# The first half of a unit's values rounded in two pieces around the next unit's first snapshot

## The chip, the cores and the metric

The kernel runs on one core of one Trainium2 chip. The metric is the device time of one execution in microseconds (us), as the median of several runs. Five engines work side by side, each through its own list of instructions in order: TensorE (PE in the rows; its weight loads are listed apart as PEld), VectorE (DVE), ScalarE (ACT), GpSimd (POOL) and SyncE (SP), which issues transfers.

## The reference

Attention with a squared rectifier, gated by `u`, is followed by two networks of two matrix products each:

```python
scores = (1.0 / S) * np.matmul(z, z.transpose(0, 2, 1))
x = u * np.matmul(np.maximum(scores, 0.0) ** 2, v)        # 2 x 3008 tokens, 256 wide
h = x @ w_in1;  g = h - np.tanh(h);  x = g @ w_out1       # 256 -> 2048 -> 256
h = x @ w_in2
g = np.where(h >= 1, h, np.where(h <= -1, 0.0, (h + 1) ** 2 / 4))
out = g @ w_out2
```

All 6016 tokens pass through both networks. The kernel's inputs are float32 (the weights of the networks arrive as float64 and are converted in the kernel).

## The kernel before, in words

After the attention both networks are worked off in units. A unit `(net, s, f)` belongs to one supertile `s` (1024 tokens, 896 in the last of six, so halves of 512 or 448 tokens) and to one of eight blocks `f` of 256 hidden features. There are 95 units, the first network's 48 ahead of the second's 47; each is one call of `Unit.emit(p)`, where `p` is the unit before. The order in which the code calls the engines is the order in which they work; nothing reorders it.

A unit makes its hidden values h with seven products instead of eight (a Strassen scheme on 2x2 blocks). Each product is three matmuls (`mult`), since every operand is held as a rounded part (`hi`) and a rest (`lo`). The seven are named in the code by their weight block: A11 and later S2, S3 and A22 are accumulated into one PSUM bank `Y`, A12 goes to `X`, S1 and S4 to `V`. Because `Y` goes on accumulating, ScalarE copies it out between products: the snapshots m1 (after A11), u2 (after S2) and u3 (after S3), all made by `snap`, shown in the trace as `m<-m` (m1) and `u<-m` (u2, u3). VectorE adds them up into h of the two halves: `ha` (first element: m1 and X; second: u3 and V) and `hb`.

Each half (class `Half`; `A` is the first, `B` the second) then goes through: `first` (in the first network the tanh, on ScalarE, tile `ta` or `tb`), `value` (on VectorE, h minus tanh, into the same tile), `round` (on ScalarE, `gha` or `ghb`, the rounded part), `rest` (on VectorE, `gla` or `glb`, the rounding's remainder). The second product (L828, `acc<-gha` and so on) is done one unit later, in pieces between the next unit's seven products, so that TensorE has work while the other engines prepare. The order on TensorE within a unit, three weight loads and matmuls for each product: A11, A12, S1, S2, then 8 with p's `gha` (4 on its element 0, 4 on its element 1), S3, 4 with `gla`, 6 with `ghb`, A22, S4, 2 with `ghb`, 4 with `glb`: 45 in all.

S2 has to wait until m1 has been copied out of `Y`, A22 until u3 has been, S4 until VectorE has read `V` (the add into `ha`'s second element).

In between, VectorE and ScalarE also do work for later: the operands of the next supertile (`xhb`, `xht`, `xhc` and their rests `xl`, the differences `t`, by `fill`), and the conversion of the next weights (`min`, `ein`, `win`, `phin`, `plin` and the like, by `work`).

A second-network unit is `late`: it rounds `gha` in the next unit, behind m1. In the first network `gha` is rounded at the unit's end (`self.A.round()`), ahead of the next unit's m1. At the second network's last supertile (`narrow`), `B.round` is made in two pieces, one ahead of u3 and one behind it; but in the second unit of that supertile (`before`, where the supertile before is also emptied) both pieces stand ahead of u3.

The line numbers are those of the profile.

Of the kernel before, what the change touches and what calls it, by code (L numbers as in the profile page):

```python
# [22 lines left out]
QT = 512  # L23
# [8 lines left out]
def attention_then_two_ffn(  # L32
# [72 lines left out]
    def flush():  # L105
        for fn in deferred:
            fn()
        deferred.clear()
# [614 lines left out]
    def fill():  # L723

        if fills:
            step = fills.pop(0)
            for fn in step:
                if fn is not None:
                    fn()
            if len(step) == 1:  # L730
                work(CONVERT[1] / 2)
        else:
            work(CONVERT[1])
        due()

    def copy(out_, in_):
        nc.scalar.activation(out=out_, in_=in_, func=AF.Copy)  # L737

    def add(out_, x, bank):
        nc.vector.tensor_tensor(out=out_, in0=x, in1=bank, op=ALU.add)  # L740
# [54 lines left out]
    class Unit:  # L795
# [60 lines left out]
        def emit(self, p, att=None):  # L856

            w = self.w
            before = p and p.net == 1 and p.f == 0 and p.s and p.before
            self.before = p  # L860
            self.late = self.net == 1 or att is not None
            one, two, three = p.parts_list if p else ([], [], [])
            narrow = self.net == 1 and w < QT
            Y = self.bank()
            self.mult(Y, A11, "b11", True)
            split = p and p.net == 1 and p.w < QT
            border = p and p.net == 1 and p.f == 0 and not before
            tight = border or narrow
            if split:
                p.A.round((0,))  # L870
            m1 = self.snap("m1", Y)
            if p and p.late:
                p.A.round((1,) if split else (None,), more=split)
            if p and p.before and p.before.net == 0:
                p.before.empty(0, leave=(1, 1) if p.net == 1 else None)
            X = self.bank()
            self.mult(X, A12, "b21", True)
            if p:
                if p.net == 1:
                    p.B.first()  # L880
                    if p.before and p.before.net == 0:
                        p.before.empty(0, late=((1, 1),))
                p.A.rest()
                p.B.first() if p.net == 0 else p.B.square(1 if before else None)
            if att:
                for fn in att[2][:5]:
                    fn()
            self.A = Half(self.net, w, "a")
            if not (p and p.late):
                add(self.A.h[:, 0, :w], m1, X[:, :w])  # L890
            V = self.bank()
            self.mult(V, S1, "t1", True)
            if att:
                for fn in att[2][5:]:
                    fn()
                got = []
                inside.append(lambda: self.mult(Y, S2, "t2"))
                inside.append(lambda: got.append(self.snap("u2", Y)))
                att[0]()
                u2 = got[0]  # L900
            else:
                if split and not before:
                    for fn in one[:2]:
                        fn()
                    one = one[2:]
                self.mult(Y, S2, "t2")
                u2 = self.snap("u2", Y)
            if before:
                before.empty(1, lambda: p.B.square(0), after=int(narrow))
            if p:  # L910
                for j in (1, 0) if before or border else (None,):
                    p.B.value(j)
                if p.late:
                    add(self.A.h[:, 0, :w], m1, X[:, :w])
            for fn in one[:4] if before else one:
                fn()
            if p:
                opening = before or p.net == 0 and p.f == 0 and p.w < QT
                p.B.round((1, 0) if opening else (1,) if tight else (None,))
                if self.i <= 1:  # L920
                    scales.pop()()
                    due()
                    due()
                elif not tight:
                    fill()
                if not tight:
                    p.B.rest()
            self.mult(Y, S3, "t3")
            if before:
                for fn in one[4:6] + two[:2] + one[6:]:  # L930
                    fn()
                two = two[2:]
            u3 = self.snap("u3", Y)
            if tight and not opening:
                p.B.round((0,), more=True)
            add(self.A.h[:, 1, :w], u3, V[:, :w])
            if border:
                p.B.rest()
            if self.net == 1 or att:
                self.A.first()  # L940
            if narrow:
                p.B.rest((1, 0))
            for fn in two:
                fn()
            if att:
                self.A.value()
                att[1]()
            if self.i > 1:
                fill()
            if self.net == 1:  # L950
                self.A.square()
            self.mult(Y, A22, "t4")
            self.mult(V, S4, "b22")
            self.B = Half(self.net, w, "b")
            if self.net == 0 and not att:
                self.A.first()
            copy(self.B.h[:, 1, :w], Y[:, :w])
            if not att:
                for j in (0, 1) if narrow else (None,):
                    self.A.value(j)  # L960
            if att:
                flush()
            add(self.B.h[:, 0, :w], u2, V[:, :w])
            for fn in three:
                fn()
            if not self.late:
                self.A.round()
            if p and p.net == 1:
                p.empty(0)
            self.parts_list = self.parts()  # L970
# [178 lines left out]
    with tc.manual_schedule():  # L1149
# [130 lines left out]
        def due():  # L1280

            now = [fn for k, fn in later if k <= 0]
            later[:] = [(k - 1, fn) for k, fn in later if k > 0]
            for fn in now:
                fn()
# [73 lines left out]
        p = None  # L1359
        for i, (net, s, f) in enumerate(units):  # L1360
            if f == 0:
                more = (net, s + 1) if (net, s + 1, 0) in units else (1, 0) if net == 0 else None
# [9 lines left out]
            p = u  # L1372
# [69 lines left out]
```

## Time and profile before

| what | value |
|---|---|
| time, median of 3 runs (lowest, highest) | 1417.55 us (1416.68, 1418.51) |
| the profiled execution's own time | 1418.15 us |
| its span, first to last instruction | 1416.4 us |
| TensorE, share of the span busy | 100% |
| TensorE weight loads | 83% |
| VectorE | 88% |
| ScalarE | 71% |
| GpSimd | 8% |
| granted TensorE clock, mean | 1.000 |

The busy share of an engine is a mean over the attention, the first network and the second. [...]

### The profile page before, as it was taken

Reading aid. Unit: us, or ns where it says so; the run is one execution under the profiler, and the core shown is the slowest. Engines: PE = TensorE matmul, PEld = TensorE weight load, DVE = VectorE, ACT = ScalarE, POOL = GpSimd, SP = SyncE. Lnnn points to the kernel's source line nnn. Section 1 sums busy time; section 2 is a strip of 40 time slices with the busy share of each in tenths; the row PEclk is TensorE's granted clock in tenths of the full one; section 3 lists DMA queues with packets and bytes.
Section 4 is the critical chain, followed back from the end, with each engine's and each line's share of the span. In section 5 each row is a group of like instructions: output and inputs, shape, how many; then the busy total and the mean of one; then the engine's idle time right before and its main releaser. Section 6 shows DMA issues by size and latency. Waiting matters only on the chain.

```text
span 1416.4 us, 21868 instructions
## 1 busy us (share of the span) xinstructions
PE 1410.3 (100%) x8206; PEld 1174.9 (83%) x8206; DVE 1246.1 (88%) x1574; ACT 999.7 (71%) x1273; POOL 116.6 (8%) x170
## 2 busy tenths in 40 slices
PE   9999999999999999999999999999999999999998
PEld 7888888888888888888888889988888888888897
DVE  8889899788898989899889889989898898988887
ACT  8888758888766767667676767666666666666764
POOL 0112110022110010110201110000000000000000
PEclk9999999999999999999999999999999999999999
DMA  8789897599989557484937567572564653546632
GB/s 228 247 281 260 228 239 191 179 282 273 257 215 324 198 193 253 170 306 134 332 129 289 212 230 270 169 294 89 176 226 178 208 191 102 188 161 219 236 103 43
DMA packets 228986, 301.02 MB, mean 213 GB/s; under 512 B 110576, under 2 KB 165616, under 8 KB 228880
## 3 DMA queue, kind: packets, MB, share of 16 engines
q1 hardware_dynamic: 212032, 257.87, 57.6%
q0 software_dynamic: 11552, 41.03, 8.2%
q10 hardware_dynamic: 5296, 0.72, 0.3%
q8 instruction: 64, 1.05, 0.3%
q14 instruction: 42, 0.34, 0.1%
HBM read 225.77 MB, written 73.79 MB: 212 GB/s over the span
## 4 chain that ended last, share of the span: by engine, by line
PE 98%; SPq 1%; DVE 0%; ACT 0%; DMA 0%; issue 0%
PE acc L828 36%; PE m L809 32%; PE acc L537 17%; PE acc L526 7%; PE sc L449 4%; SPq L397 1%; PE acc L1063 0%; PE h L1011 0%; PE acc L532 0%; PE warm L1147 0%; DMA ub<-in_u_dram 0%; PE acc L554 0%; DVE am L416 0%; DVE lo L499 0%; DVE lo L434 0%
## 5 line engine op out<-in xcount | busy, mean ns | idle before, releaser
L809 PE MATMUL m<-xht,w 128*128 128x512 f32 (+1 forms) x760 | 231.5, 386 | 0.0
L828 PE MATMUL acc<-ghb,w 128*128 128x512 f32 (+1 forms) x760 | 201.2, 386 | 0.0
L537 PE MATMUL acc<-hi,v 64*128 64x512 f32 (+1 forms) x1588 | 195.4, 382 | 0.1
L828 PE MATMUL acc<-gha,w 128*128 128x512 f32 (+1 forms) x760 | 188.0, 386 | 0.0
L537 PEld LDWEIGHTS acc<-hi,v 64*128 64x128 f32 x1588 | 148.5, 184 | 28.8 <-DVE y L592 0.8
L828 PEld LDWEIGHTS acc<-ghb,w 128*128 128x128 f32 x760 | 141.6, 188 | 28.8 <-ACT ghb L737 0.2
L828 PEld LDWEIGHTS acc<-gha,w 128*128 128x128 f32 x760 | 142.6, 188 | 27.4
L809 PEld LDWEIGHTS m<-xht,w 128*128 128x128 f32 x760 | 142.7, 188 | 26.7
L809 PE MATMUL m<-xlt,w 128*128 128x512 f32 (+1 forms) x380 | 147.3, 388 | 0.0
L782 DVE TENSOR_TENSOR gla<-ta,gha 128x1024 fp32r<-128x1024 f32 (+1 forms) x95 | 114.3, 1204 | 37.4 <-ACT gha L737 36.9
L737 ACT ACTIVATE ghb<-tb 128x1024 fp32r<-128x1024 f32 (+3 forms) x108 | 101.4, 944 | 59.7 <-DVE tb L768 59.2
L768 DVE TENSOR_TENSOR ta<-ha,ta 128x1024 f32<-128x1024 f32 (+2 forms) x102 | 114.4, 1127 | 27.4 <-ACT ta L764 22.3
L737 ACT ACTIVATE u<-m 128x512 f32<-128x512 f32 (+1 forms) x190 | 110.5, 581 | 30.9 <-PE m L809 30.0
L782 DVE TENSOR_TENSOR glb<-tb,ghb 128x1024 fp32r<-128x1024 f32 (+3 forms) x102 | 114.5, 1128 | 15.1 <-ACT ghb L737 14.8
L737 ACT ACTIVATE gha<-ta 128x1024 fp32r<-128x1024 f32 (+2 forms) x101 | 100.1, 991 | 38.3 <-DVE ta L768 37.9
L768 DVE TENSOR_TENSOR tb<-hb,tb 128x1024 f32<-128x1024 f32 (+3 forms) x101 | 114.8, 1137 | 7.2 <-ACT tb L753 2.6
L809 PE MATMUL m<-xhb,w 128*128 128x512 f32 (+1 forms) x380 | 115.7, 386 | 0.0
L537 PE MATMUL acc<-lo,v 64*128 64x512 f32 (+1 forms) x772 | 104.8, 382 | 0.2 <-DVE lo L434 0.2
L475 ACT ACTIVATE r<-sc 128x1024 f32<-128x1024 f32 (+1 forms) x83 | 84.4, 1017 | 28.7 <-PE sc L449 28.3
L764 ACT ACTIVATE ta<-ta 128x1024 f32<-128x1024 f32 (+1 forms) x47 | 49.1, 1046 | 78.6 <-DVE ta L755 78.6
L828 PE MATMUL acc<-gla,w 128*128 128x512 f32 (+1 forms) x380 | 101.5, 386 | 0.0
L828 PE MATMUL acc<-glb,w 128*128 128x512 f32 (+1 forms) x380 | 101.5, 386 | 0.0
(139 smaller groups left out, 2569.8 us busy)
## 6 DMA issues: line engine op xcount, KB each, us to landing
w<-packed SPq DMA_DIRECT2D x288, 512.0 KB, 5.9
mir<-ax SPq DMA_DIRECT2D x50, 512.0 KB, 4.6
m<-mir SPq DMA_DIRECT2D x200, 128.0 KB, 4.7
xr<-kept SPq DMA_DIRECT2D x20, 512.0 KB, 6.8
packed<-phin POOLq DMA_DIRECT2D x16, 512.0 KB, 5.8
packed<-plin POOLq DMA_DIRECT2D x16, 512.0 KB, 6.2
widein<-in_moe_w_in_dram POOLq DMA_DIRECT2D x15, 512.0 KB, 6.4
wideout<-in_moe_w_out_dram POOLq DMA_DIRECT2D x15, 512.0 KB, 7.4
```

Of the source, the lines that this page charges most:

```text
L397: nc.sync.dma_start(out=m[32 * i : 32 * i + 32, :k].rearrange("b k t a -> b k (t a)"), in_=src[:, :k, 256 * i + 128 * h : 256 * i + 128 * ...
L449: nc.tensor.matmul(ps[:, j, :n], zs[b, g][half, x, k0 : k0 + P], q[half, y, :n], start=(k == 0), stop=(k == 2))
L475: nc.scalar.activation(out=r[s], in_=ps[s], func=AF.Relu)
L526: nc.tensor.matmul(acc[d][h].rearrange("p (i q) -> p i q", i=2), lhsT, g[half, j], start=start, stop=stop)
L537: nc.tensor.matmul(acc[d][h][:, :n], lhsT, g[half, j, :n], start=start, stop=stop and (h == 1 or not closes))
L737: nc.scalar.activation(out=out_, in_=in_, func=AF.Copy)
L764: nc.scalar.activation(out=t, in_=t, func=AF.Square, scale=0.5, bias=0.5)
L768: nc.vector.tensor_tensor(out=t, in0=self.h[self.at(j)], in1=t, op=ALU.subtract if self.net == 0 else ALU.max,)
L782: nc.vector.tensor_tensor(out=self.lo[s], in0=self.t[s], in1=self.hi.bitcast(F32)[s], op=ALU.subtract)
L809: nc.tensor.matmul(bank[:, : self.w], self.win[wp][:, block, :], xop[self.net, self.s][x][xp], start=start and i == 0, stop=True, skip_gro ...
L828: nc.tensor.matmul(self.acc(d, n)[:, : self.w], self.wout[:, part, j, d * P : (d + 1) * P], g[:, at, : self.w], start=start, stop=stop,)
```

## The change

For every first-network unit but the first of each supertile (`halved`; six supertiles times seven blocks make 42 units), `A.round()` at the unit's end makes element 0 only, and the next unit makes element 1 behind its m1. Each half costs an instruction of its own on ScalarE; the remainder `gla` (`p.A.rest()`) is still one instruction for both elements. The next units are those with f from 2 to 7 and, behind each supertile, the one with f = 0. In the second network, the unit `(1, 5, 1)` makes the second piece of `B.round` behind u3, not ahead of it.

```diff
@@ Unit.emit
             m1 = self.snap("m1", Y)
             if p and p.late:
                 p.A.round((1,) if split else (None,), more=split)
+            elif p and p.halved:
+                p.A.round((1,), more=True)
...
             if p:
-                opening = before or p.net == 0 and p.f == 0 and p.w < QT
+                opening = before and not narrow or p.net == 0 and p.f == 0 and p.w < QT
                 p.B.round((1, 0) if opening else (1,) if tight else (None,))
...
+            self.halved = not self.late and self.f > 0
             if not self.late:
-                self.A.round()
+                self.A.round((0,) if self.halved else (None,))
```

ScalarE, first network, from the end of one unit into the next (the unit whose timeline stands in the rows further down has the same order of names), before:

```order
L737 ACTIVATE hb<-m 128x512
L737 ACTIVATE gha<-ta 128x1024
L737 ACTIVATE m_7005<-m 128x512
L753 ACTIVATE tb<-hb 128x1024
L737 ACTIVATE u_7024<-m 128x512
L737 ACTIVATE ghb<-tb 128x1024
L679 ACTIVATE xht_1_7038<-t_1_6886 128x1024
L737 ACTIVATE u_7045<-m 128x512
L753 ACTIVATE ta<-ha 128x1024
```

and with the change:

```order
L737 ACTIVATE hb<-m 128x512
L737 ACTIVATE gha<-ta 128x512
L737 ACTIVATE m_7010<-m 128x512
L737 ACTIVATE gha<-ta 128x512
L753 ACTIVATE tb<-hb 128x1024
L737 ACTIVATE u_7030<-m 128x512
L737 ACTIVATE ghb<-tb 128x1024
L679 ACTIVATE xht_1_7044<-t_1_6890 128x1024
L737 ACTIVATE u_7051<-m 128x512
L753 ACTIVATE ta<-ha 128x1024
```

One rounding of 1024 columns ahead of the snapshot `m` has become one of 512 ahead of it and one of 512 behind it; the tanh `tb` stands behind both. VectorE's order at the same place is the same in both kernels; with the change it reads:

```order
L740 TENSOR_TENSOR hb<-u_6943,m 128x512
L782 TENSOR_TENSOR gla<-ta,gha 128x1024
L740 TENSOR_TENSOR ha<-m_7010,m 128x512
L768 TENSOR_TENSOR tb<-hb,tb 128x1024
L695 TENSOR_TENSOR xhc_1_6958<-xr_1_1_6370,xhc_1_6958 128x512
L782 TENSOR_TENSOR glb<-tb,ghb 128x1024
L740 TENSOR_TENSOR ha<-u_7051,m 128x512
```

Nothing moved here: `gla`, which reads all of `gha`, still stands ahead of the add into `ha` and of the value `tb`.

ScalarE in the second network's unit `(1, 5, 1)`, before:

```order
L764 ACTIVATE tb<-tb 128x448
L737 ACTIVATE ghb<-tb 128x448 x2
L737 ACTIVATE u_14517<-m 128x448
L764 ACTIVATE ta<-ta 128x2x448
L737 ACTIVATE hb<-m 128x448
```

and with the change:

```order
L764 ACTIVATE tb<-tb 128x448
L737 ACTIVATE ghb<-tb 128x448
L737 ACTIVATE u_14558<-m 128x448
L737 ACTIVATE ghb<-tb 128x448
L764 ACTIVATE ta<-ta 128x2x448
```

The second of the two pieces has moved behind the snapshot u3.

## Rows read from the trace of the kernel before

**Rows 1.** The page: engine busy times, and the chain that ended last.

```profile
PE 1410.3 (100%) x8206; PEld 1174.9 (83%) x8206; DVE 1246.1 (88%) x1574; ACT 999.7 (71%) x1273; POOL 116.6 (8%) x170
...
PE 98%; SPq 1%; DVE 0%; ACT 0%; DMA 0%; issue 0%
```

**Rows 2.** Waits, S2 behind m1: total us, times, longest us.

```profile
PEld m L809 <- ACT m L737: 0.6, 2, 0.4
```

**Rows 3.** Timeline of ScalarE, one first-network unit: start us, us, instruction, idle before.

```profile
488.83 1.06 ACT L737 ACTIVATE gha<-ta 128x1024 fp32r<-128x1024 f32 x1 [0.38 <-DVE ta L768]
490.51 0.60 ACT L737 ACTIVATE m<-m 128x512 f32<-128x512 f32 x1 [0.62 <-PE m L809]
491.01 1.05 ACT L753 ACTIVATE tb<-hb 128x1024 f32<-128x1024 f32 x1
...
493.35 1.06 ACT L737 ACTIVATE ghb<-tb 128x1024 fp32r<-128x1024 f32 x1 [0.20 <-DVE tb L768]
494.32 1.04 ACT L679 ACTIVATE xht<-t 128x1024 fp32r<-128x1024 f32 x1
495.27 0.58 ACT L737 ACTIVATE u<-m 128x512 f32<-128x512 f32 x1
```

**Rows 4.** Timeline of VectorE, the same unit.

```profile
489.93 1.23 DVE L782 TENSOR_TENSOR gla<-ta,gha 128x1024 fp32r<-128x1024 f32 x1 [0.53 <-ACT gha L737]
...
492.09 1.23 DVE L768 TENSOR_TENSOR tb<-hb,tb 128x1024 f32<-128x1024 f32 x1
...
495.88 0.69 DVE L740 TENSOR_TENSOR ha<-u,m 128x512 f32<-128x512 f32 x1 [0.20 <-ACT u L737]
496.48 0.68 DVE L658 TENSOR_TENSOR t<-xr,t 128x512 f32<-128x512 f32 x1
...
497.69 1.23 DVE L768 TENSOR_TENSOR ta<-ha,ta 128x1024 f32<-128x1024 f32 x1
498.84 0.68 DVE L740 TENSOR_TENSOR hb<-u,m 128x512 f32<-128x512 f32 x1
```

**Rows 5.** Timeline of the weight loads, the same unit (consecutive ones merged, xcount).

```profile
489.41 0.19 PEld L809 LDWEIGHTS m<-xlb,w 128*128 128x128 f32 x1
...
495.53 1.32 PEld L828 LDWEIGHTS acc<-ghb,w 128*128 128x128 f32 x6
496.89 0.19 PEld L809 LDWEIGHTS m<-xlt,w 128*128 128x128 f32 x1
...
497.57 0.64 PEld L809 LDWEIGHTS m<-xhc,w 128*128 128x128 f32 x3
```

**Rows 6.** Groups of ScalarE by form: busy us, mean ns, idle before.

```profile
L286 ACT ACTIVATE phout<-wout 128x512 fp32r<-128x512 f32 x16 | 9.9, 620 | 1.1 <-DVE wout L270 1.1
```

**Rows 7.** Timeline of a second-network unit: ScalarE's round, TensorE's load behind it.

```profile
967.12 1.06 ACT L737 ACTIVATE ghb<-tb 128x1024 fp32r<-128x1024 f32 x1 [1.00 <-DVE tb L768]
...
968.24 1.25 PEld L828 LDWEIGHTS acc<-ghb,w 128*128 128x128 f32 x6
```

**Rows 8.** Timeline of the weight loads around a late m1 (first network).

```profile
593.13 0.41 PEld L809 LDWEIGHTS m<-xht,w 128*128 128x128 f32 x2
593.98 0.19 PEld L809 LDWEIGHTS m<-xlt,w 128*128 128x128 f32 x1 [0.43 <-ACT m L737]
...
594.56 1.79 PEld L828 LDWEIGHTS acc<-gha,w 128*128 128x128 f32 x8
```

**Rows 9.** Timeline of VectorE in the unit ahead of that, full of conversions.

```profile
585.17 0.68 DVE L263 SCALAR_TENSOR_TENSOR min<-widein,min 128x512 f32<-128x512 uint32 x1
...
587.10 1.22 DVE L782 TENSOR_TENSOR glb<-tb,ghb 128x1024 fp32r<-128x1024 f32 x1
...
588.83 0.51 DVE L250 TENSOR_SCALAR eout<-wideout 128x512 uint32<-128x512 uint32 x1
...
591.15 1.21 DVE L768 TENSOR_TENSOR ta<-ha,ta 128x1024 f32<-128x1024 f32 x1
```

**Rows 10.** Timeline of the weight loads in the unit (1, 5, 1).

```profile
1346.93 0.19 PEld L809 LDWEIGHTS m<-xlt,w 128*128 128x128 f32 x1 [0.22 <-ACT u L737]
```

## The prediction

> **What bounds the kernel now.** I read the page first: TensorE is busy for the whole span, and the chain that ended last runs through it for 98% [rows 1]. So neither VectorE's nor ScalarE's busy share matters in itself; what matters is whether a weight load of TensorE is held back. The waits say how little there is to win where the change aims: S2's load waited for the snapshot m1 twice in the whole kernel, 0.6 us in all [rows 2]. Then I read one undisturbed first-network unit on three engines, the one whose first weight load stands at 489.41 (call this T0) [rows 3 to 5]. Six loads take 1.36 us [rows 5], so one takes 0.227 us and a unit of 45 takes 10.20 us. The reader should look for three things. ScalarE idles 0.62 us ahead of m1, until TensorE has finished A11 [rows 3]. VectorE idles 0.53 us ahead of `gla`, until `gha` is rounded [rows 4]. And the load of `ghb` at 495.53 [rows 5] comes 1.12 us after the rounding that it needs (493.35 + 1.06 = 494.41 [rows 3]): that is the unit's slack on this path, and it shows no idle time.
>
> **How much lateness costs nothing.** The row at 593.13 merges two loads, so the next, S2's first, was due at 593.13 + 2 x 0.227 = 593.58. It waited for m1 and came at 593.98, 0.40 late. The load three further on was due at 594.26 and came at 594.56, 0.30 late [rows 8]. So 0.10 us of lateness of a load is made up for and the rest is lost; I count each stall as its lateness less 0.10.
>
> **The change, part by part.** *First piece of `gha`.* In the unit at T0 it takes 0.62 us in place of 1.06 (a rounding of 512 columns [rows 6]) and starts at 488.83 as before [rows 3]. It is done at 489.45, but m1 waits for TensorE until 490.51 either way. Gain: nothing, in any unit where m1 already waits for TensorE. Where `gha` is late, m1 comes up to 0.5 us earlier; rows 2 bound what that is worth at 0.6 us together.
>
> *Second piece, behind m1.* The next place on ScalarE is 0.50 us behind m1's start (490.51 to 491.01, today the tanh's [rows 3]). The piece stands there from 491.01 to 491.63. The tanh `tb` moves to 491.51 and ends at 492.56. ScalarE can spare that, but VectorE works in order and `gla` needs both pieces. It starts 0.04 us behind the rounding's end (489.89 to 489.93 [rows 3, 4]), so at 491.67, 1.74 later than now. Behind it stand the add into `ha` and the value `tb`. A 1024-column operation is followed by the next 1.15 us later (497.69 to 498.84), a 512-column one 0.60 us later (495.88 to 496.48) [rows 4]: `ha` at 492.82, `tb` at 493.42 in place of 492.09. The rounding of `ghb` starts 1.26 us behind that (492.09 to 493.35 [rows 3, 4]): 494.68, done at 495.74. A load starts 0.06 us behind the rounding it waits for (967.12 + 1.06 = 968.18, then 968.24 [rows 7]): 495.80, where 495.53 was its turn. It is 0.27 late and 0.17 is lost. This repeats: m1 hangs on TensorE's own A11, so every unit starts the same chain afresh, and no slack is carried over. Of the 42 units 35 are of full width for `gha`: 35 x 0.17 = 6.0 us. The seven behind halves of 448 tokens are not in my rows; between 0 and 7 x 0.17 = 1.2, I take the middle, 0.6.
>
> *What that makes late next.* ScalarE's own work behind `ghb` moves by 1.33 us too. Where an operand's rounding of 1024 columns stands between, u3 starts 0.97 + 0.95 us behind `ghb` (493.35, 494.32, 495.27 [rows 3]): 496.60, done at 497.18, A22's load at 497.24. Its turn would be 496.89 + 0.17 = 497.06: 0.08 lost. VectorE reads u3 and `V` 0.03 later for 0.69 us [rows 3, 4], done at 497.90, S4's load at 497.96 in place of 497.57 + 0.25 = 497.82: 0.04 lost. Together 0.12 us, in 21 units: three such roundings for each of the six operand sets that this network prepares, and three units (at 591, 755 and 912 us) in which a conversion's `phin` stands there. 2.5 us. Without such a rounding u3 is done at 496.23, in time.
>
> *Where VectorE is full of conversions.* S2's first load is a unit's tenth, 2.04 us behind its start; the unit of [rows 8] started at 593.58 - 2.04 = 591.54, and the one before it, that of [rows 9], at 581.34. Take these two. `tb` at T0 + 4.01 = 585.35; 1.15 on, the conversions between it and `glb` take 1.93 (585.17 to 587.10), so `glb` stands at 588.43 and the add into `ha` at 589.57, done 590.26. S4's load at 590.32 was due at 589.50 + 0.17: 0.55 lost. Another 2.32 of conversions (588.83 to 591.15) put `ta` at 592.49; its first piece is rounded at 593.76, m1 ends 1.10 later, S2's load comes at 594.92 and not at 594.30: 0.52 lost (today 0.30 [rows 8]). The second piece starts at 594.76, and by the chain above (491.01 to 495.80) the load of `ghb` comes at 599.55 where 598.90 was its turn: 0.55 lost. The pair loses 1.79 us, 1.15 more than twice 0.17 and today's 0.30. This is the heaviest pair; the conversions come in all shapes. Below it is 0 (elsewhere VectorE regains its time in front of `gla`), above it is one such pair for each supertile, 7 us. I take 4.
>
> *Unit (1, 5, 1).* A22's load idles 0.22 us for u3 [rows 10], 0.04 of which is the usual gap between loads. Moving a piece of `ghb` behind u3 frees at most 0.18 - 0.10, so 0.1 us once.
>
> The sum: 6.0 + 0.6 + 2.5 + 4.0 - 0.1 = 13.0 us. The profiled execution took 1418.15 us, 1.75 of it outside its span and untouched, and is 0.6 above the median: 1431.15, as a median 1430.5.
>
> **A rule against the row.** The wait of rows 7 and 8 stands on the weight load itself, and the load came late with its operand. The Trainium skill, "TensorE: Matmul & The Clock Gate", section "Step-by-step: what each phase is for", says that TensorE pulls weight loads ahead of matmuls in flight, the matmuls alone keeping their order. By that only the matmul would wait for `ghb`, and the sum would be about half of mine. The rows here show the load held, so I keep 0.10.
>
> **The rivals.** *Lateness is mostly hidden* (more of it free than one stall shows). If the load went ahead and only the matmul waited, a matmul's turn is 0.227 behind its load's: 495.76 for `ghb`, ready at 495.80. 35 x 0.04 = 1.4 us; at u3 0.08 in 21 units, 1.7; of the conversions 3. Some 6 us: 1423.5. For it: the free 0.10 is read from one stall only. Against: that stall is of the same kind. This is what the Trainium skill's rule named above would make of the change.
>
> *Heavier.* VectorE does not regain its time between two units full of conversions, and two such pairs come in a supertile: 14 in place of 4, with the other terms 23 us, 1440; in part of this case some 1437. For it: VectorE is 88% busy [rows 1], and the change forces it to stand idle for `gla` each time. Against: it had idle time before `gla` to give, 0.53 us in the unit read [rows 4].
>
> *Not slower.* The chain would have to bring `ghb` 0.17 us sooner per unit than I add up: 0.10 late or less and every such stall is free. A second piece that takes 0.45 us in place of 0.62 would do. Then the earlier m1 is all that is left, up to 0.6 us: 1417. For it: all my steps are sums of gaps of 0.03 to 0.06 us, six of them. Against: each is read from a row. That the split does not happen is excluded by the order of ScalarE's instructions.
>
> **How the numbers follow.** The forecast has a chance of 0.58 (its own range 1426 to 1436), mostly hidden 0.16, heavier 0.14, not slower 0.12. Faster by over 0.2% (2.8 us, about what a measurement of this kernel can tell from no change) would need more than all that S2 waits for: 0.01. Within 0.2%: the rest of that case and a little of the hidden one, 0.12. Slower: 0.87. The range 1421 to 1437 leaves out the case that is not slower and half of the heavier.
>
> **What would show it.** In the changed kernel's profile: TensorE's loads of `ghb` idle for ScalarE's `ghb` in most first-network units, some 0.3 us each, in place of none; VectorE idles about 1 us for `gha` ahead of `gla`; `tb` on VectorE starts about 4.0 us behind the unit's first load (2.7 today); undisturbed units last 10.35 to 10.5 us, not 10.20; the attention and the second network are unchanged. If units still last 10.20 us with `tb` at 4.0, my price of a late load is wrong; if `tb` comes earlier, the chain on VectorE is.

## The result, and the profile after

| | before | changed |
|---|---|---|
| time, median of 4 runs each | 1417.84 us | 1434.30 us (1433.86 to 1434.44) |
| span of the profiled execution | 1416.4 us | 1432.6 us |

The ratio is 1.0118 (95% interval 1.0106 to 1.0130): slower by 16.5 us.

The page's chain of the changed kernel, beside [rows 1]:

```profile
PE 86%; DVE 9%; ACT 3%; issue 2%; DMA 0%; SPq 0%; DVEq 0%; ACTq 0%
```

Before, the chain ran through TensorE for 98%. Now 12% of it are VectorE and ScalarE: the chain turns to them wherever TensorE waited for them. That share, 172 us of the span, says where the chain runs and not how much was lost. The waits of the changed kernel say for what an engine waited (total us, times, longest us):

```profile
DVE gla L782 <- ACT gha L737: 67.9, 87, 1.5
...
PEld acc L828 <- ACT ghb L737: 16.1, 45, 0.7
...
PEld m L809 <- DVE ha L740: 6.6, 28, 0.7
...
PEld m L809 <- ACT u L737: 5.9, 26, 0.5
...
PEld m L809 <- ACT m L737: 4.4, 9, 1.0
```

The first two of these waits in the kernel before:

```profile
DVE gla L782 <- ACT gha L737: 36.9, 82, 1.0
PEld acc L828 <- ACT ghb L737: 0.2, 1, 0.2
```

The load of `ghb`, which waited once for 0.2 us before, waits 45 times: in all 42 units behind a divided one and in three with f = 1. The wait of S2 for m1, which had been 0.6 us in two times [rows 2], has grown to 4.4 us in nine. In seven of them m1 has only half a rounding ahead of it; the other two, 1.3 us together, are units with f = 1, where the rounding ahead of m1 is whole.

The loss lies in the first network. Its third unit starts at 458.86 us (458.81 before); from there to the second network's first load it takes 479.15 us in place of 462.89, 16.3 us more.

The unit of [rows 3 to 5] in the changed kernel; its first weight load stands at 490.45. ScalarE's timeline:

```profile
490.83 0.64 ACT L737 ACTIVATE gha<-ta 128x512 fp32r<-128x512 f32 x1 [0.81 <-DVE ta L768]
491.55 0.60 ACT L737 ACTIVATE m<-m 128x512 f32<-128x512 f32 x1
492.04 0.62 ACT L737 ACTIVATE gha<-ta 128x512 fp32r<-128x512 f32 x1
492.56 1.05 ACT L753 ACTIVATE tb<-hb 128x1024 f32<-128x1024 f32 x1
...
495.69 1.06 ACT L737 ACTIVATE ghb<-tb 128x1024 fp32r<-128x1024 f32 x1 [1.50 <-DVE tb L768]
496.66 1.04 ACT L679 ACTIVATE xht<-t 128x1024 fp32r<-128x1024 f32 x1
497.60 0.58 ACT L737 ACTIVATE u<-m 128x512 f32<-128x512 f32 x1
```

VectorE's timeline:

```profile
492.70 1.22 DVE L782 TENSOR_TENSOR gla<-ta,gha 128x1024 fp32r<-128x1024 f32 x1 [1.30 <-ACT gha L737]
493.84 0.68 DVE L740 TENSOR_TENSOR ha<-m,m 128x512 f32<-128x512 f32 x1
494.44 1.22 DVE L768 TENSOR_TENSOR tb<-hb,tb 128x1024 f32<-128x1024 f32 x1
```

and the weight loads:

```profile
490.45 0.19 PEld L809 LDWEIGHTS m<-xlb,w 128*128 128x128 f32 x1
...
496.80 1.22 PEld L828 LDWEIGHTS acc<-ghb,w 128*128 128x128 f32 x6 [0.27 <-ACT ghb L737]
498.23 0.19 PEld L809 LDWEIGHTS m<-xlt,w 128*128 128x128 f32 x1 [0.21 <-ACT u L737]
498.95 0.54 PEld L809 LDWEIGHTS m<-xhc,w 128*128 128x128 f32 x3 [0.19 <-DVE ha L740]
...
500.92 0.19 PEld L809 LDWEIGHTS m<-xlb,w 128*128 128x128 f32 x1
```

Put the three lists together in order of time. VectorE idles 1.30 us until the second piece of `gha` is there (492.04 + 0.62), then works through `gla`, the add and the value without a pause; ScalarE idles 1.50 us for that value; TensorE idles 0.27 us for `ghb`. Behind the operand's rounding `xht`, u3 is late too, and with it A22 and S4: three short waits in one unit. Some whole units, as windows (length in us; busy us and instructions of TensorE, its weight loads, VectorE, ScalarE and GpSimd; granted clock; busy share of the DMA engines; GB/s):

```profile
490.45:500.92 10.47, 10.47 (x47) 8.22 (x45) 8.96 (x11) 7.31 (x10) 0.05 (x1) 1.00 0.61 227
500.92:511.27 10.35, 10.35 (x47) 8.37 (x46) 9.03 (x11) 6.88 (x10) 0.00 (x0) 1.00 0.37 106
532.10:543.49 11.39, 10.81 (x47) 8.13 (x46) 11.25 (x15) 7.99 (x11) 1.13 (x3) 1.00 0.88 268
585.89:596.79 10.90, 10.66 (x46) 8.29 (x45) 9.51 (x14) 6.36 (x9) 3.53 (x5) 1.00 0.40 141
596.79:608.09 11.30, 10.90 (x47) 8.14 (x46) 9.46 (x12) 7.11 (x10) 1.14 (x3) 1.00 0.99 373
```

The second is the plain case, 10.35 us in place of 10.20; the first has an operand's rounding ahead of u3, 10.47; the other three are full of conversions, and the one from 532.10 is a unit with f = 1. Note that TensorE's busy time in the first two still fills the unit: the stalls hide in the modelled ends of the matmuls, and show only in the length of the unit and in the loads' idle time.

### The profile page after: what moved, and what is told of

It reads as the page before. It is cut to its first block, busy times and chain, and to the rows that moved or that the text cites. A ratio compares the mean times of both kernels' runs of the same rounds, so it can differ in the third digit from the quotient of the medians.

```text
span 1432.6 us, 21910 instructions
## 1 busy us (share of the span) xinstructions
PE 1422.9 (99%) x8206; PEld 1167.3 (81%) x8206; DVE 1241.7 (87%) x1574; ACT 994.1 (69%) x1315; POOL 114.5 (8%) x170
## 4 chain that ended last, share of the span: by engine, by line
PE 86%; DVE 9%; ACT 3%; issue 2%; DMA 0%; SPq 0%; DVEq 0%; ACTq 0%
PE acc L828 30%; PE m L809 26%; PE acc L537 17%; PE acc L526 7%; PE sc L449 4%; DVE tb L768 2%; DVE gla L782 2%; DVE ha L740 1%; ACT gha L737 1%; DVE ta L768 1%; ACT ghb L737 1%; DVE glb L782 1%; PE acc L1066 0%; PE h L1014 0%; PE acc L532 0%
## 5 line engine op out<-in xcount | busy, mean ns | idle before, releaser
L828 PE MATMUL acc<-ghb,w 128*128 128x512 f32 (+1 forms) x760 | 207.3, 394 | 1.9 <-ACT ghb L737 1.7
L828 PEld LDWEIGHTS acc<-ghb,w 128*128 128x128 f32 x760 | 138.1, 188 | 42.6 <-ACT ghb L737 16.1
L737 ACT ACTIVATE gha<-ta 128x512 fp32r<-128x512 f32 (+3 forms) x143 | 108.3, 757 | 54.8 <-DVE ta L768 54.8
```

The lines of the kernel that those rows point to most:

```text
L828: nc.tensor.matmul(self.acc(d, n)[:, : self.w], self.wout[:, part, j, d * P : (d + 1) * P], g[:, at, : self.w], start=start, stop=stop,)
```

## The experiments

Theory: VectorE works in order, so `gla` holds the add and the value `tb` back until the second piece is rounded behind m1; that makes `ghb` late on TensorE. Rivals: ScalarE's 42 extra instructions and the later tanh cost the time; or the loss in units full of conversions is carried on from unit to unit by the change itself. Each kernel is compared with the kernel before in runs on the same chip.

**half_only.** The first part of the change alone: from the diff, without the line on `opening`.

> The first part of the change alone (first half rounded in two pieces in the first network; the second network as before). Theory, that VectorE waits for the second piece: all of the loss and more, since the second network's units (1,5,1) and behind ran 1.2 us faster with the whole change: 1.2 us above the changed kernel, about 1435.5 us; undisturbed first-network units last 10.35 us. Rival, that this gain came from the first network by some phase of TensorE's stream: the same time as the changed kernel, 1434.3.

Measured: 1435.84 us, ratio 1.0127 (1.0113 to 1.0141). The first part makes the whole loss. The time expected, 1435.5 us, came, but the reason given for the 1.2 us above the whole change is not shown (**before_again**), so that part of the hit counts as luck. The 1.5 us measured there come from two separate comparisons.

**piece_only.** The second part alone, the changed line on `opening`.

> The second part alone (the unit (1,5,1) rounds its second piece behind u3). Theory: the five narrow units from (1,5,1) on last 9.12 us in place of 9.30 and the end is 0.4 us shorter: 1.2 us faster than before, about 1416.6 us. Rival: only the one wait in front of A22 goes, 0.1 us.

Measured: 1416.90 us against 1417.82, ratio 0.9995 (0.9986 to 1.0004): not told from no change. In its trace the unit (1, 5, 1) lasts 9.23 us in place of 9.39, since A22 no longer waits for u3.

**add_first.** The whole change, and VectorE's add ahead of `gla`:

```diff
-                p.A.rest()
+                if not p.halved:
+                    p.A.rest()
...
                 add(self.A.h[:, 0, :w], m1, X[:, :w])
+            if p and p.halved:
+                p.A.rest()
```

> The whole change, but VectorE makes the add into ha ahead of the remainder gla. Theory (VectorE's order): ha 1.85 us behind the unit's first load, gla 2.45, value tb 3.60, rounding of ghb 4.85, done 5.91, its load's turn is 6.12: no stall in undisturbed units, 10.20 us again; only units full of conversions still lose something, in all 0 to 5 us over before, 1417 to 1422. Rival (ScalarE's extra instruction and the later tanh cost the time): still some 16 us slower than before.

Measured: 1419.71 us, ratio 1.0014 (1.0005 to 1.0022). Two instructions of VectorE change places and 14.6 of the 16.5 us are gone, with ScalarE's list the same to the last instruction. VectorE in one of its units, whose first load stands at 489.88:

```profile
491.72 0.69 DVE L740 TENSOR_TENSOR ha<-m,m 128x512 f32<-128x512 f32 x1 [1.04 <-PE m L809]
492.33 1.22 DVE L782 TENSOR_TENSOR gla<-ta,gha 128x1024 fp32r<-128x1024 f32 x1
493.46 1.22 DVE L768 TENSOR_TENSOR tb<-hb,tb 128x1024 f32<-128x1024 f32 x1
```

The add now uses the time in which `gha`'s second piece is rounded, and `tb` stands 3.58 us behind the unit's start (3.99 in the changed kernel). The unit lasts 10.20 us. This shows the wait of `gla` as the cause. It clears the extra instructions, and the later tanh too, which starts 2.12 us behind the unit's start here and 2.11 in the changed kernel. The 1.9 us that are left are clear of no change; in the trace 27 of the first network's 38 full-width units from its third on last 10.20 us, and the two longest, 11.11 and 10.84, are full of conversions.

**whole_behind.** No pieces: the whole rounding behind m1.

```diff
             elif p and p.halved:
-                p.A.round((1,), more=True)
+                p.A.round()
...
-                self.A.round((0,) if self.halved else (None,))
+            if not self.late and not self.halved:
+                self.A.round()
```

> The whole rounding of the first half behind m1, in one piece, for the same units (no extra instruction). Theory: gla waits 0.44 us longer than with two pieces, the load of ghb comes 0.70 late and not 0.25, so undisturbed units last 10.80 us and 42 units lose 0.45 more: some 19 us over the changed kernel, 1453. Rival (the extra instruction costs): faster than the changed kernel, near 1418 to 1425.

Measured: 1445.95 us, ratio 1.0199 (1.0184 to 1.0215): 28 us slower than before, with not one instruction more. Plain units last 10.8 us as expected; the load of `ghb` in the unit from 491.68, which has an operand's rounding too:

```profile
498.47 1.01 PEld L828 LDWEIGHTS acc<-ghb,w 128*128 128x128 f32 x5 [0.71 <-ACT ghb L737]
```

The time expected was 7 us too high; it put 0.45 us more on all 42 units. Where conversions fill VectorE the two delays did not add: with nothing of `gha` ahead of m1 in the 42 next units, S2's waits for m1 are 1.3 us in two times, both in units with f = 1, and not 4.4 in nine. What makes up the rest of the 7 us was not taken apart.

**both_ahead.** The kernel before, with both pieces ahead of m1.

```diff
-                self.A.round()
+                self.A.round((0, 1) if self.f > 0 else (None,))
```

> The kernel before with the first half's rounding in two pieces, both ahead of m1, in the same 42 units (the same 42 extra instructions, nothing moved behind m1). Theory (the place behind m1 costs, not the second instruction): the two pieces end 0.1 us later than the one, undisturbed units stay at 10.20 us, 0 to 1.5 us slower than before in all. Rival (the extra instruction): a good part of the 16 us.

Measured: 1417.35 us against 1417.12, ratio 1.0002 (0.9993 to 1.0011). Two instructions in place of one cost nothing that can be measured; the place behind m1 does.

**before_add_first.** The kernel before with the order of add_first, `gha` undivided and ahead of m1 (`swap` is true where the changed kernel has `halved`).

```diff
-                p.A.rest()
+                swap = p.net == 0 and p.f > 0
+                if not swap:
+                    p.A.rest()
...
                 add(self.A.h[:, 0, :w], m1, X[:, :w])
+            if p and swap:
+                p.A.rest()
```

> The kernel before with VectorE's add into ha ahead of gla in the 42 units, the rounding undivided and ahead of m1. Theory: gla then starts 2.45 us behind the unit's first load whether the second piece is late or not (it would be there at 2.22), so undisturbed units stay at 10.20 us and the time is within 1.5 us of the same order with the split, 1418.5 to 1421. Rival (the split itself still costs there): equal to the kernel before, some 2 us less than the order with the split.

Measured: 1425.17 us, ratio 1.0055 (1.0042 to 1.0068). Neither expectation held. The later `tb` moves everything behind it, `ta` too, so that `gha` comes late and, in one piece, holds m1 back: VectorE's add waits for m1 36 times, 35.9 us together (12 times and 7.0 us in add_first). S2's waits for m1 in this kernel, and then in add_first:

```profile
PEld m L809 <- ACT m L737: 8.3, 15, 1.1
```

```profile
PEld m L809 <- ACT m L737: 2.7, 7, 0.7
```

So the division does relieve m1 (5.6 us less of this wait), once VectorE has fallen behind. In the kernel before it hardly had (0.6 us of this wait [rows 2]).

**rest_too.** The whole change, with `gla` in two pieces as well, the second behind the value `tb`:

```diff
...
-                p.A.rest()
+                p.A.rest((0,) if p.halved else (None,))
...
                     p.B.value(j)
+                if p.halved:
+                    p.A.rest((1,), more=True)
```

> The whole change, and the remainder gla is divided as well: its first element where gla stood, its second behind VectorE's value tb. Theory: nothing on VectorE then waits for the second piece ahead of the add and the value; the value starts when the tanh is done, 3.20 us behind the unit's first load, ghb is rounded by 5.52, its load's turn is 6.12: undisturbed units 10.20 us; 42 instructions more on VectorE; in all 0.5 us faster to 2 us slower than before, 1417 to 1419.5. Rival (an order in which gla is whole is needed, or the instruction count costs): above the 1419.7 of the order with the add first.

Measured: 1420.43 us, ratio 1.0020 (1.0012 to 1.0029). The plain units last 10.20 us, as the theory said, and no load of `ghb` waits for long (0.8 us in three times). But units full of conversions still lose 2 to 3 us together, 1 us more than I allowed for. The time is above the 1419.7 us that the rival had named; whether the 42 extra instructions of VectorE make that or their order was not taken apart.

**before_one_set** and **after_one_set.** The kernel before and the changed kernel without the second network's weight conversions; the second network is run with the first one's weights.

```diff
+        net = 0
         assert {(net, f, "in"), (net, f, "out")} <= done
...
+            if net:
+                continue
             converts.append(convert(net, f, "in", ...))
```

> The kernel before without the conversion of the second network's weights: that network is run with the first one's weights, so 16 conversions are left out of the first network's units. Theory: nothing waited there but about 1 us: 1415 to 1418.

> The changed kernel with the same conversions left out (the second network is run with the first one's weights). Theory: the loss that is left is that of undisturbed units, 35 x 0.15, and of the units with an operand's rounding, 18 x 0.11, and that of the narrow units, about 1: 8 to 9 us more than the kernel before with the same left out, and not 16; the units behind f = 0 (f = 1) lose nothing. Rival (the loss in the heavy units is not the conversions' but the change's own, carried from unit to unit): still some 15 us.

Measured: 1416.23 and 1424.40 us; between them 8.2 us (by the spans, 1413.8 and 1422.5, 8.7). Without the conversions half of the loss is gone, and S2 waits for m1 in neither kernel. What is left (waits of after_one_set, whose lines are shifted by one):

```profile
PEld acc L829 <- ACT ghb L738: 11.1, 41, 0.4
...
PEld m L810 <- ACT u L738: 5.0, 22, 0.5
...
PEld m L810 <- DVE ha L741: 4.6, 21, 0.5
```

That is the plain chain: `ghb` in 41 units, u3 and the add behind it in some 20 (7 and 6 in before_one_set). The full-width units with f = 1 last 10.20 us, as expected. So the other half comes only with the conversions and is not something that the change carries on by itself. The pair takes out all of a conversion's work at once, VectorE's, ScalarE's and the transfers, and does not tell which of it costs.

**before_again** and **piece_again.** The kernel before and piece_only, profiled once more.

> The kernel before once more, to see whether the pace of the 448-column units repeats: in the second network's narrow units 9.30 us as in the first profile if the three stalls in (1,5,1) set it, either 9.30 or 9.12 if it is chance.

> The second part alone once more: in the second network's narrow units behind (1,5,1) 9.12 us again if the missing stalls set the pace; either value if it is chance. In the first network's narrow units, where the code is that of before, either value.

Measured: in the second network's narrow units behind (1, 5, 1) both last 9.12 us, in the first network's 9.12 (before_again) and 9.30 (piece_again). The same code ran at either pace: the second network's units at 9.30 us in the first profile of the kernel before and at 9.12 in the second. So the better pace does not need the change, and my reason for the 1.2 us in half_only and piece_only is not shown. In all seven profiles with the second part the second network's narrow units were at 9.12, in those without it three times at 9.12 and three times at 9.30; whether the second part makes the better pace likelier stays open.

## Why the prediction was right, point by point

Forecast were 1430.5 us (1421 to 1437) and 13.0 us more than before; measured 1434.3 and 16.5. Direction, place and mechanism held; one term of the sum, that of the units full of conversions, was too small.

- **What bounds the kernel.** Held: the unit is 45 loads of TensorE, and only a late load costs. The busy shares of VectorE and ScalarE hardly moved (88% to 87%, 71% to 69%) while 16 us were lost.
- **The first piece gains nothing where m1 waits for TensorE.** Held in the plain units. That it gains up to 0.5 us for m1 where `gha` is late was true of the place and not of the sum: VectorE falls behind, `gha` comes later, and S2 waits more than before. That every unit starts the same chain afresh held by little: in the unit shown the first piece starts 0.38 us behind the unit's first load, where the whole rounding had started 0.58 ahead of it [rows 3], and ends at 491.47, 0.08 us before m1. A rounding of 1.06 us in its place would have ended 0.34 us after m1's start (an estimate from these rows). So the first piece, which the prediction puts at nothing, keeps m1 in time here.
- **The chain behind the second piece.** Held within 0.04 us: `gla` 2.25 us behind the unit's start (forecast 2.26), `tb` 3.99 (4.01), the load of `ghb` 6.35 (6.39). Plain units last 10.35 us: 0.15 lost, forecast 0.17; 35 x 0.15 = 5.3 us for 6.0.
- **What a late load costs.** Lateness less 0.10 held: 0.24 late (an idle time of 0.27, less the usual gap), 0.15 lost. The rule of the Trainium skill, "TensorE: Matmul & The Clock Gate", section "Step-by-step: what each phase is for", that weight loads are pulled ahead of matmuls in flight, does not help here, where the load's own matmul lacks its operand: the load itself shows the wait, in all 42 units. Whether TensorE holds the load or the program's wait stands on it, the trace does not tell.
- **u3 and S4 behind an operand's rounding.** Held: 10.47 against 10.35, 0.12 us, as forecast.
- **Units full of conversions.** The mechanism held and its size was off; this is the term of the sum that was mis-sized. The pair that was worked out came close to its forecast: 10.90 + 11.30 us, less 10.20 and 10.51, is 1.49 more, and the sum had 1.79 less today's 0.30. Its four stalls were there in order (two small ones, 0.20 for u3 and 0.19 for `ha`, belong to the term on u3, so the pair came 0.12 below what the terms make together):

```profile
592.25 1.23 PEld L828 LDWEIGHTS acc<-ghb,w 128*128 128x128 f32 x6 [0.28 <-ACT ghb L737]
594.82 0.53 PEld L809 LDWEIGHTS m<-xhc,w 128*128 128x128 f32 x3 [0.66 <-DVE ha L740]
599.40 0.19 PEld L809 LDWEIGHTS m<-xlt,w 128*128 128x128 f32 x1 [0.59 <-ACT m L737]
604.00 1.23 PEld L828 LDWEIGHTS acc<-ghb,w 128*128 128x128 f32 x6 [0.65 <-ACT ghb L737]
```

  I then took 4 us for all such stretches, with 7 as the upper end; by the pair of kernels without conversions it is 16.2 - 8.7 = 7.5 us of span, above that end. The stretches were read from one pair and their number guessed. Left out altogether were the units with f = 1, which are not divided themselves but stand behind one that has run late: the unit from 532.10 lasts 11.39 us (10.26 before), since a whole rounding and a late `ta` hold its m1, and with it S2:

```profile
535.10 0.19 PEld L809 LDWEIGHTS m<-xlt,w 128*128 128x128 f32 x1 [1.00 <-ACT m L737]
```

  The four full-width units with f = 1 that stand behind a late one last 1.8 us longer together.
- **The narrow units.** A little too small: the one from 899.58 lasts 9.27 us, where 9.12 is the pace of its loads (see below), so 0.15 is lost as in a wide unit. The six in the first network make 0.9 us (an estimate from this one), where 0.6 stood for seven.
- **Unit (1, 5, 1).** Forecast 0.1 us; the unit lasts 0.16 us less where only this part is changed. In the whole time that can't be told from nothing.
- **The rivals.** Not slower and mostly hidden are out: the plain unit's 0.15 alone is above what the first allows, and the second had 0.04. The heavier one was right in part: VectorE does fall behind from one unit to the next in places, and the conversions cost 7.5 us, between the 4 of the forecast and its own 14.

## What to carry to other kernels

An instruction that is moved behind another is priced by who waits for it, in that engine's own order: here a 0.6 us rounding, moved in 42 units, on an engine with nearly a third of its time free cost 16 us, because the engine that reads it stands in line with everything that follows. If a producer is divided to be out of the way sooner, its reader has to be moved or divided too, and even that gained nothing here (1.9 and 2.9 us slower than before); alone, the division costs nothing (two pieces at the old place) and gains nothing. And a stall worked out in a clean unit should be counted again in the fullest one, unit by unit, before a share of them is guessed.

## What the hardware showed unexpectedly

Weight loads and matmuls of 448 columns run at two paces, with the same code. Eight loads in a row in the first network's last supertile, in the first profile of the kernel before (one unit and the next):

```profile
886.98 1.63 PEld L828 LDWEIGHTS acc<-gha,w 128*128 128x128 f32 x8
...
896.28 1.63 PEld L828 LDWEIGHTS acc<-gha,w 128*128 128x128 f32 x8
```

and in the second profile of the same kernel:

```profile
886.99 1.60 PEld L828 LDWEIGHTS acc<-gha,w 128*128 128x128 f32 x8
...
896.11 1.61 PEld L828 LDWEIGHTS acc<-gha,w 128*128 128x128 f32 x8
```

A unit of 45 lasts 9.30 us at one pace and 9.12 at the other, 0.18 us apart, none of these rows shows a wait in either, and the granted clock is 1.00 in both; over the narrow units of both networks that is some 2 us of an execution. What decides it was not found.
